# Seeding an accumulation bank from ScalarE in a Strassen-style up projection (one Trainium2 core)

## The chip, the core and the metric

The kernel runs on one core of a Trainium2 chip. The core has a matrix engine (TensorE, PE in the rows, with its weight loads as PEld), a vector engine (VectorE, DVE), an activation engine (ScalarE, ACT), GpSimd (POOL), and SyncE (SP), which here only starts transfers. Each engine runs its own instructions in order and waits for the others by semaphores. Matrix products land in PSUM, which holds eight banks of 128 x 512 fp32; everything else lives in SBUF or in HBM. The metric is the device time of one execution in microseconds (us).

## The reference

Three parts run one after the other on 3072 tokens of width 512: a retention layer, and two feed-forward networks of inner width 2048.

```python
for t in range(S):
    state = gamma * state + k_t v_t^T
    y[:, :, t] = scale * q_t state
x = y as (3072, 512)
h = x @ w_in;   g = h / (1 + exp(-1.702 * h));   x = g @ w_out       # moe, l = 0
h = x @ w_in2;  g = max(h, 0) ** 2;              out = g @ w_out2    # moe2, l = 1
```

All matrices are fp32. The kernel keeps that precision by splitting each operand into a high and a low part (fp32r) and taking three products: low weight by high x, high weight by high x, high weight by low x.

## The kernel before

**Stages.** The retention comes first. Then two blocks of 512 tokens go through the first network in the plain way. The other tokens go in *blocks* (l, n) of 1024 tokens (l is the network): (0,1), whose up projection is still plain, then (0,2), (1,0), (1,1), (1,2). Each block has an up stage and a down stage. The four blocks after (0,1) run their up stage in `up2`; all five run their down stage in `down2`.

**Seven products.** Both stages use a Strassen-Winograd scheme: a 2 x 2 block product is made of seven products instead of eight, from sums of quarters of the weights and of x. In `up2` the outer loop is over rounds p = 0 to 7 (NQ = 8), one for each strip of 128 inner columns, and one call past the end (p = 8) that finishes round 7. A product is six matmuls of 128 x 128 by 128 x 512. The quarters of the result, named 11, 12, 21 and 22, are SBUF tiles `g[q, p // 2]`, reached by `gt(q, p)`.

**The order in a round.** Product 1 goes into bank X, which ScalarE copies to quarter 11 (L882, through the helper at L864). Then products 4 and 3 of the round before finish quarters 21 and 12 (L887, L896); in round 0 there is no round before, and this part is skipped. Product 2 opens bank Y (L904, L905). VectorE adds Y to quarter 11 (L906, through the helper at L869). Product 6 accumulates onto X, copied to quarter 12 (L909); product 5 opens bank Z; product 7 accumulates onto X again, copied to quarter 22 (L913), to which Z is added (L914). The eight bank numbers stand in a deque: `bank` takes one from its left, and a free one goes back on its right.

**The activation.** `add` queues gelu, or relu and square, in `late`; the next `copy` on ScalarE runs what is queued, right behind itself. In blocks (1,1) and (1,2) VectorE does relu squared itself (L876). Quarter 21 is finished by product 4 alone and gets its activation straight from the bank (L890, L892, L893).

**What else is in the queues.** `background` (L903, L916) issues pieces of a weight maker: while (0,2) and (1,0) run, it makes the weight sums of the second network out of raw weights, with ScalarE scalings and casts (L129, L130, L383), VectorE sums, and GpSimd transfers to HBM (L346). `prepare` (L946, L947) splits operands of the down stage; it is called in rounds 6 and 7. SP fetches the weights of every product from HBM into eight slots (L761), each refilled when its product is through. `loads` (L1059) brings the next block's x from HBM at the start of a down stage. The order on every engine is the order of the program (`manual_schedule`).

Of the kernel before, what the change touches and what calls it, by code (L numbers as in the profile page):

```python
# [15 lines left out]
ACTF = mybir.ActivationFunctionType  # L16
# [44 lines left out]
def tile_retention_then_two_ffns(  # L61
# [10 lines left out]
    nc = tc.nc  # L72
# [336 lines left out]
    def background(us):  # L409

        credit[0] += us
        while acts:
            acts.popleft()()
        while credit[0] > 0:
            c = next(maker, None)
            if c is None:
                credit[0] = min(credit[0], 3.0)
                return
            credit[0] -= c
# [21 lines left out]
    with tc.manual_schedule():  # L441
# [310 lines left out]
        def fetch():  # L752
            while queue and len(fetched) < SLOTS:
                l, n, m, i, p = key = queue[0]
                if turn[0] % SLOTS >= len(wr_p):
                    return
                assert key[:1] + key[2:3] + key[4:] in made
                queue.popleft()
                t = wr_p[turn[0] % SLOTS].tile([P, 2, 256], F32R, tag="w", name="r{}_{}_{}_{}_{}".format(*key))
                turn[0] += 1  # L760
                nc.sync.dma_start(out=t.bitcast(F32), in_=kw[l][m][p][PRODUCT[i][0]])  # L761
                fetched[key] = t
# [21 lines left out]
        banks = deque(range(8))  # L784
# [48 lines left out]
        def thirds(m):  # L833

            t = g[12, m]
            v.tensor_tensor(out=t, in0=g[22, m], in1=t, op=ALU.subtract)

        def bank(name):
            k = banks.popleft()
            return ps_p[0].tile([P, TB], F32, tag=f"b{k}", name=name), k  # L840

        def matmul(a, w, b, start, stop):
            nc.tensor.matmul(a, w, b, start=start, stop=stop, skip_group_check=True)  # L843

        def up2(l, n, first):

            xb, yb, zb = {}, {}, {}
            late = deque()

            def product(i, p, a, start):  # L850
                s, b = PRODUCT[i]
                w = fetched.pop((l, n, 0, i, p)).rearrange("p k (h c) -> p k h c", h=2)
                for k in range(2):
                    hi, lo = w[:, k, 0], w[:, k, 1]
                    matmul(a, lo, xh[b][:, k], start and k == 0, False)
                    matmul(a, hi, xh[b][:, k], False, False)
                    matmul(a, hi, xl[b][:, k], False, k == 1)
                fetch()

            def gt(q, p):  # L860
                return g[q, p // 2][:, p % 2]

            def copy(t, a):
                nc.scalar.copy(out=t, in_=a)  # L864
                while late:
                    late.popleft()()

            def add(t, a):
                v.tensor_tensor(out=t, in0=a, in1=t, op=ALU.add)  # L869
                if l == 0:  # L870
                    late.append(lambda: nc.scalar.activation(out=t, in_=t, func=ACTF.Gelu_apprx_sigmoid))
                elif n == 0:
                    late.append(lambda: nc.scalar.activation(out=t, in_=t, func=ACTF.Relu))
                    late.append(lambda: nc.scalar.activation(out=t, in_=t, func=ACTF.Square))
                else:
                    v.scalar_tensor_tensor(out=t, in0=t, scalar=0.0, in1=t, op0=ALU.max, op1=ALU.mult)  # L876

            for p in range(NQ + 1):
                if p < NQ:
                    xb[p] = bank(f"X{l}_{n}_{p}")  # L880
                    product(1, p, xb[p][0], True)
                    copy(gt(11, p), xb[p][0])  # L882
                else:
                    next(first)
                if p > 0:
                    a, k = xb.pop(p - 1)
                    product(4, p - 1, a, False)  # L887
                    t = gt(21, p - 1)
                    if l == 0:
                        nc.scalar.activation(out=t, in_=a, func=ACTF.Gelu_apprx_sigmoid)  # L890
                    else:
                        nc.scalar.activation(out=t, in_=a, func=ACTF.Relu)  # L892
                        nc.scalar.activation(out=t, in_=t, func=ACTF.Square)  # L893
                    banks.append(k)
                    a, k = zb.pop(p - 1)
                    product(3, p - 1, a, False)  # L896
                    add(gt(12, p - 1), a)
                    banks.append(k)
                    if p == NQ - 1:
                        prepare(l, n)  # L900
                if p < NQ:
                    if (l, n) != blocks[-1] and p < NQ - 1:
                        background(BGUP[l])  # L903
                    yb = bank(f"Y{l}_{n}_{p}")  # L904
                    product(2, p, yb[0], True)  # L905
                    add(gt(11, p), yb[0])  # L906
                    banks.append(yb[1])
                    product(6, p, xb[p][0], False)
                    copy(gt(12, p), xb[p][0])  # L909
                    zb[p] = bank(f"Z{l}_{n}_{p}")  # L910
                    product(5, p, zb[p][0], True)
                    product(7, p, xb[p][0], False)
                    copy(gt(22, p), xb[p][0])  # L913
                    add(gt(22, p), zb[p][0])  # L914
                    if (l, n) != blocks[-1] and p < NQ - 1:
                        background(BGUP[l])  # L916
                if p == NQ:
                    while late:
                        late.popleft()()
                if p > 1 and p % 2 == 0:  # L920
                    thirds(p // 2 - 1)
                if p == NQ - 2:
                    prepare(l, n)
# [6 lines left out]
        def prepare(l, n):  # L930

            if not todo:
                return
            i, m = todo.popleft()
            k = places[0]
            places[0] += 1
            hi, lo = (
                pool.tile([P, 2, TB], F32R, tag=tag, name=f"gx{l}_{n}_{i}_{m}_{e}")
                for e, (pool, tag) in enumerate(
                    ((wa_p, "w0"),) * 2 if k < 3 else  # L940
                    ((wa_p, "w0"), (wb_p, "w0")) if k % 3 == 2 else ((hl_p, "hl"),) * 2
                )
            )

            src = g[{1: 11, 2: 21, 6: 11, 5: 11, 7: 12, 4: 21, 3: 22}[i], m]
            nc.scalar.copy(out=hi, in_=src)  # L946
            v.tensor_tensor(out=lo, in0=src, in1=hi, op=ALU.subtract)  # L947
            ready.append((i, m, hi, lo))
# [96 lines left out]
        for k, (l, n) in enumerate(blocks):  # L1045
            todo.extend((i, m) for i in ORDER for m in range(NQ // 2))
            gen = [iter(())]

            xt = []

            def loads(u):

                if k + 1 == len(blocks):
                    return
                t, i = divmod(u, 2)
                b, j = blocks[k + 1]
                if i == 0:
                    xt.append(block_tiles(f"xb{b}_{j}_{t}"))
                nc.gpsimd.dma_start(out=xt[t][i], in_=(xkept, ykept)[b][2 * j + t][:, 2 * i:2 * i + 2])  # L1059
                if u == 3:  # L1060
                    gen[0] = x_operands(*xt)

            rest = down2(l, n, loads, lambda: next(gen[0], None))
            if (l, n) == plain:
                up_plain()
            else:
                up2(l, n, rest)
            for _ in rest:
                pass
            for _ in gen[0]:  # L1070
                pass
            if (l, n) == (1, 0):
                assert next(maker, 0) == 0 and not acts
# [83 lines left out]
```

## Time and profile before

| | us |
|---|---|
| three runs of the kernel before | 1041.03, 1043.52, 1044.09 |
| their median | 1043.52 |
| the profiled execution | 1041.52 |
| its span, first to last instruction | 1039.8 |
| TensorE busy | 1028.8 (99%) |
| VectorE busy | 762.5 (73%) |
| ScalarE busy | 559.1 (54%) |
| HBM traffic | 263 GB/s over the span |

Matmuls overlap one another: one starts every 0.227 us and its row lasts 0.39 us, so TensorE's busy time counts rows that run together and is no measure of its peak. What holds TensorE up is better read from its waits. The other engines' busy times are averages over stages that differ; a stage's own share is read from windows of the timeline.

### The profile page before, as it was taken

The numbers are of one execution on the slowest core, as the hardware profiler recorded it, in microseconds if no ns is written. First come the engines' busy times: TensorE is split into PE (matmuls) and PEld (weight loads), VectorE is DVE, ScalarE is ACT, GpSimd is POOL, SyncE is SP. The second block draws the span as 40 slices with busy tenths as digits, with TensorE's granted clock in tenths as the row PEclk, the third lists the DMA queues.
The fourth block names the chain that finished last, engine by engine and source line by source line (L and its number), as shares of the span: only waits on it lengthen the run. The fifth ranks groups of instructions, "written<-read, shape, count | busy, mean of one in ns | idle before, by whom it ended". The sixth has DMA issues, their size and how long they took to land.

```text
span 1039.8 us, 15581 instructions
## 1 busy us (share of the span) xinstructions
PE 1028.8 (99%) x5602; PEld 849.1 (82%) x5602; DVE 762.5 (73%) x1059; ACT 559.1 (54%) x906; POOL 119.7 (12%) x183
## 2 busy tenths in 40 slices
PE   9999999999999999999999999999999999999998
PEld 6888888888888888888788888788888888888886
DVE  5798998798898888567787566887445986355953
ACT  4677775344766365556455688464233464234442
POOL 3121210111333000112000111000100001000000
PEclk9999999999999999999999999999999999999999
DMA  9995898865898867999867898767866667776664
GB/s 348 404 404 174 270 313 298 308 229 223 268 349 286 312 208 227 329 338 351 276 213 229 309 369 299 272 210 236 296 193 194 203 204 229 219 194 193 207 198 162
DMA packets 114637, 274.04 MB, mean 264 GB/s; under 512 B 12160, under 2 KB 12288, under 8 KB 114304
## 3 DMA queue, kind: packets, MB, share of 16 engines
q1 hardware_dynamic: 87008, 171.32, 50.0%
q0 software_dynamic: 26976, 100.67, 27.6%
q8 instruction: 45, 0.74, 0.3%
q10 hardware_dynamic: 576, 1.05, 0.3%
q14 instruction: 32, 0.26, 0.1%
HBM read 199.59 MB, written 73.40 MB: 263 GB/s over the span
## 4 chain that ended last, share of the span: by engine, by line
PE 82%; DMA 2%; DVE 0%; issue 0%
PE D L843 36%; PE X L843 16%; PE Z L843 8%; PE Y L843 4%; PE h L797 3%; PE h L795 3%; PE h L796 3%; DMA r<-kw 2%; PE y L676 2%; PE y L674 2%; PE y L675 2%; PE h L643 2%; PE h L645 1%; PE h L644 1%; DVE o L981 0%
## 5 line engine op out<-in xcount | busy, mean ns | idle before, releaser
L843 PE MATMUL D<-gx,r 128*128 128x512 f32 x1680 | 383.7, 390 | 2.9 <-DMA r<-kw 2.9
L843 PEld LDWEIGHTS D<-gx,r 128*128 128x128 f32 x1680 | 314.7, 188 | 70.8 <-DMA r<-kw 4.6
L947 DVE TENSOR_TENSOR gx<-g,gx 128x1024 fp32r<-128x1024 f32 x140 | 170.6, 1221 | 49.8 <-ACT gx L946 49.2
L946 ACT CAST gx<-g 128x1024 fp32r<-128x1024 f32 x140 | 145.1, 1050 | 110.2 <-PE D L843 97.4
L843 PE MATMUL X<-xh,r 128*128 128x512 f32 x512 | 157.7, 389 | 0.0
L864 ACT COPY g<-X 128x512 f32<-128x512 f32 x96 | 56.3, 586 | 154.6 <-PE X L843 154.4
L869 DVE TENSOR_TENSOR g<-Z,g 128x512 f32<-128x512 f32 x64 | 44.2, 691 | 123.0 <-ACT g L864 93.6
L843 PEld LDWEIGHTS X<-xh,r 128*128 128x128 f32 x512 | 96.0, 188 | 20.1 <-ACT g L864 0.2
L843 PE MATMUL X<-xl,r 128*128 128x512 f32 x256 | 99.6, 389 | 0.0
L843 PE MATMUL Z<-xh,r 128*128 128x512 f32 x256 | 78.8, 389 | 0.0
L843 PEld LDWEIGHTS Z<-xh,r 128*128 128x128 f32 x256 | 48.0, 188 | 10.0
L843 PEld LDWEIGHTS X<-xl,r 128*128 128x128 f32 x256 | 48.1, 188 | 10.0
L643 PE MATMUL h<-hl,w 128*128 128x512 f32 x128 | 50.2, 392 | 0.4 <-DVE w L167 0.4
L644 PE MATMUL h<-hl,w 128*128 128x512 f32 x128 | 49.9, 390 | 0.0
L645 PE MATMUL h<-hl,w 128*128 128x512 f32 x128 | 49.8, 389 | 0.0
L676 PE MATMUL y<-gl,w 128*128 128x512 f32 x128 | 49.8, 389 | 0.0
L674 PE MATMUL y<-gh,w 128*128 128x512 f32 x128 | 49.8, 389 | 0.0
L675 PE MATMUL y<-gh,w 128*128 128x512 f32 x128 | 49.8, 389 | 0.0
L795 PE MATMUL h<-hl,w 128*128 128x512 f32 x128 | 49.8, 389 | 0.0
L796 PE MATMUL h<-hl,w 128*128 128x512 f32 x128 | 49.8, 389 | 0.0
L797 PE MATMUL h<-hl,w 128*128 128x512 f32 x128 | 49.8, 389 | 0.0
L843 PE MATMUL Z<-xl,r 128*128 128x512 f32 x128 | 49.8, 389 | 0.0
(107 smaller groups left out, 1604.5 us busy)
## 6 DMA issues: line engine op xcount, KB each, us to landing
r<-kw SPq DMA_DIRECT2D x504, 256.0 KB, 3.0
kw<-wq POOLq DMA_DIRECT2D x32, 896.0 KB, 6.5
unit<-qkv SPq DMA_DIRECT2D x48, 512.0 KB, 9.0
raw<-w POOLq DMA_DIRECT2D x32, 512.0 KB, 6.3
kw<-wh POOLq DMA_DIRECT2D x16, 1024.0 KB, 4.7
kw<-w SPq DMA_DIRECT2D x16, 512.0 KB, 5.0
raw<-win POOLq DMA_DIRECT2D x16, 512.0 KB, 6.5
raw<-wout POOLq DMA_DIRECT2D x16, 512.0 KB, 7.2
```

Source lines behind the costliest of these rows:

```text
L643: nc.tensor.matmul(hp, lo[:, k], xh, start=(k == 0), stop=False)
L644: nc.tensor.matmul(hp, hi[:, k], xh, start=False, stop=False)
L645: nc.tensor.matmul(hp, hi[:, k], xl, start=False, stop=(k == KD - 1))
L674: nc.tensor.matmul(a, lo[:, e], gh, start=s0, stop=False)
L675: nc.tensor.matmul(a, hi[:, e], gh, start=False, stop=False)
L676: nc.tensor.matmul(a, hi[:, e], gl, start=False, stop=s1)
L795: nc.tensor.matmul(hp, lo[:, k], xh, start=(k == 0), stop=False)
L796: nc.tensor.matmul(hp, hi[:, k], xh, start=False, stop=False)
L797: nc.tensor.matmul(hp, hi[:, k], xl, start=False, stop=(k == KD - 1))
L843: nc.tensor.matmul(a, w, b, start=start, stop=stop, skip_group_check=True)
L946: nc.scalar.copy(out=hi, in_=src)
L947: v.tensor_tensor(out=lo, in0=src, in1=hi, op=ALU.subtract)
```

## The change

Product 1 goes into X as before, but ScalarE copies it into the bank of product 2, Y, which is now taken ahead of the copy. Product 2 no longer opens that bank: its first matmul accumulates onto what ScalarE wrote. ScalarE then reads the finished sum from Y and writes quarter 11 through gelu, or through relu and a square in place; VectorE's addition, its relu squared in blocks (1,1) and (1,2), and the queued activation of quarter 11 go.

```diff
                 if p < NQ:
                     xb[p] = bank(f"X{l}_{n}_{p}")
                     product(1, p, xb[p][0], True)
-                    copy(gt(11, p), xb[p][0])
+                    yb[p] = bank(f"Y{l}_{n}_{p}")
+                    copy(yb[p][0], xb[p][0])
                 else:
                     next(first)
@@
                 if p < NQ:
                     if (l, n) != blocks[-1] and p < NQ - 1:
                         background(BGUP[l])
-                    yb = bank(f"Y{l}_{n}_{p}")
-                    product(2, p, yb[0], True)
-                    add(gt(11, p), yb[0])
-                    banks.append(yb[1])
+                    a, k = yb.pop(p)
+                    product(2, p, a, False)
+                    t = gt(11, p)
+                    if l == 0:
+                        nc.scalar.activation(out=t, in_=a, func=ACTF.Gelu_apprx_sigmoid)
+                    else:
+                        nc.scalar.activation(out=t, in_=a, func=ACTF.Relu)
+                        nc.scalar.activation(out=t, in_=t, func=ACTF.Square)
+                    banks.append(k)
                     product(6, p, xb[p][0], False)
```

## Rows read from the trace of the kernel before

**Rows 1.** The page: span, then busy us, share of it, instructions.
```profile
span 1039.8 us, 15581 instructions
...
PE 1028.8 (99%) x5602; PEld 849.1 (82%) x5602; DVE 762.5 (73%) x1059; ACT 559.1 (54%) x906; POOL 119.7 (12%) x183
```

**Rows 2.** Waits of PE and, in 576:640, PEld: waiter, released by: us, times, longest.
```profile
PE D L843 <- DMA r<-kw: 2.9, 4, 1.0
...
PEld X L843 <- ACT g L864: 0.2, 1, 0.2
```

**Rows 3.** Chain that ended last, in order: start us, us, what.
```profile
422.82 1.36 PE Y L843 x6
...
432.34 1.36 PE Y L843 x6
...
492.21 10.23 DMA r<-kw
```

**Rows 4.** Groups by line and form: count, busy us, mean ns, idle before.
```profile
L864 ACT COPY g<-X 128x512 f32<-128x512 f32 x96 | 56.3, 586 | 154.6 <-PE X L843 154.4
...
L869 DVE TENSOR_TENSOR g<-Y,g 128x512 f32<-128x512 f32 x32 | 22.0, 687 | 4.4 <-PE Y L843 4.2
...
L437 ACT CAST hl<-x 128x512 fp32r<-128x512 f32 x12 | 6.5, 617 | 0.0
```

**Rows 5.** Timeline, round 0 of (0,2): start us, us, what, [idle before <-releaser].
```profile
422.43 0.39 PE L843 MATMUL X<-xl,r 128*128 128x512 f32 x1
...
422.65 0.62 PE L843 MATMUL Y<-xh,r 128*128 128x512 f32 x2
...
422.85 0.59 ACT L864 COPY g<-X 128x512 f32<-128x512 f32 x1 [8.69 <-PE X L843]
```

**Rows 6.** Timeline, ScalarE, round 0 of blocks (1,0) and (1,2).
```profile
577.10 0.59 ACT L864 COPY g<-X 128x512 f32<-128x512 f32 x1 [8.69 <-PE X L843]
...
884.40 0.59 ACT L864 COPY g<-X 128x512 f32<-128x512 f32 x1 [8.69 <-PE X L843]
```

**Rows 7.** Timeline, (1,0): ScalarE's copy, the weight load and matmul behind it.
```profile
630.60 0.57 ACT L864 COPY g<-X 128x512 f32<-128x512 f32 x1
...
631.22 0.30 PEld L843 LDWEIGHTS X<-xh,r 128*128 128x128 f32 x2 [0.18 <-ACT g L864]
...
631.30 0.65 PE L843 MATMUL X<-xh,r 128*128 128x512 f32 x2
```

**Rows 8.** Timeline: round 7 of (0,2), and a copy in (1,0).
```profile
488.82 0.58 ACT L864 COPY g<-X 128x512 f32<-128x512 f32 x1
...
489.29 0.62 PE L843 MATMUL Y<-xh,r 128*128 128x512 f32 x2
...
594.66 0.56 ACT L864 COPY g<-X 128x512 f32<-128x512 f32 x1
```

**Rows 9.** Timeline, (1,0): round 3's scaling and product 7; round 4's pair.
```profile
607.56 0.68 ACT L130 ACTIVATE raw<-raw 128x512 uint32<-128x512 uint32 x1
...
609.54 0.62 PE L843 MATMUL X<-xh,r 128*128 128x512 f32 x2
...
614.15 0.58 ACT L892 ACTIVATE g<-X 128x512 f32<-128x512 f32 x1
...
615.30 0.93 ACT L383 CAST wq<-w 128x896 fp32r<-128x896 f32 x1
```

**Rows 10.** Windows of the up stages of (1,0), (1,1): us, busy us, PEclk, DMA.
```profile
575.60:646.50 70.90, 70.90 (x314) 58.61 (x313) 47.08 (x88) 58.25 (x98) 13.33 (x19) 1.00 0.95 333
730.40:806.60 76.20, 76.20 (x338) 63.10 (x337) 38.59 (x53) 25.48 (x41) 2.98 (x6) 1.00 0.75 228
```

**Rows 11.** DMA issues in 480:490 and 490:494 (us to landing); timeline of GpSimd.
```profile
r<-kw SPq DMA_DIRECT2D x8, 256.0 KB, 5.8
...
r<-kw SPq DMA_DIRECT2D x3, 256.0 KB, 10.2
...
488.78 0.94 POOL L346 DMA_DIRECT2D kw<-wq  x1 [7.27 <-DVE wq L345]
489.72 2.18 POOL L1059 DMA_DIRECT2D xb<-ykept  x4
```

## The prediction

> **What bounds the kernel now.** I read the page's first part, then the table of who waited for whom, filtered to TensorE, then the chain of waits in order of time, and last the timeline around one up stage. The page [rows 1] shows TensorE busy for 99% of the span and ScalarE for 54%. Busy TensorE rows overlap, so that 99% proves little by itself. The waits do: the matmuls wait 2.9 us in total, always for a weight fetch, four times [rows 2], and in the up stages one weight load waits once, 0.2 us, for ScalarE. The chain [rows 3] shows the rest: product after product without a gap, 1.36 us each (six matmuls), and one round of seven products every 9.52 us (from the Y product of round 0 at 422.82 to that of round 1 at 432.34). So TensorE's stream sets the end. VectorE and ScalarE work beside it; taking work off VectorE gains nothing unless TensorE waited for it, and any wait put into the stream is added to the span in full.
>
> **Part by part.**
>
> *VectorE's additions of product 2.* 32 go, 22.0 us of VectorE [rows 4]; in blocks (1,1) and (1,2) the 16 in-place relu squared behind them go too. No wait of TensorE in [rows 2] names them: worth nothing on the path. The cover is TensorE's own stream.
>
> *The copy, now from bank to bank.* 32 copies stay on ScalarE and only their target moves. A copy out of PSUM takes 586 ns on average, a cast of the same size that reads SBUF 617 [rows 4]. No row writes PSUM from ScalarE. I bound it by 0.53 us (0.59 less twice the 31 ns that the memory read makes) and 0.69 us (VectorE's slowest operation on this size in [rows 4], rounded), and take 0.59, the row with the same source.
> The Trainium skill, "ScalarE: Activation LUTs", section "Step-by-step: what each stage is for", says that ScalarE writes PSUM faster than SBUF. "Perfetto Trace Analysis", section "Optimizing Scalar/DVE Operations", puts ScalarE's access overhead at 93 ns on SBUF and 51 on PSUM, with the profiled latency about twice that. By these, as an estimate, the copy would take some 0.5 us and the whole sum would be about 0.3 us smaller; only the read side of it is visible in this trace.
>
> *The new wait.* This is the part that costs. Before, product 2 opened its own bank and needed nothing from ScalarE. Now its first matmul must wait until the copy has landed. Queued behind that matmul is the whole of TensorE's stream, and everyone else waits for that.
> In rounds 1 to 7 products 4 and 3 of the round before lie between product 1 and product 2: 2.72 us of cover for a copy of 0.59. In round 0 there is no round before: product 2 follows product 1 directly, and there are four such rounds, one for each up stage in this form. The timeline of the first [rows 5]: the last matmul of product 1 starts at 422.43 and ends at 422.82, product 2 starts at 422.65, and ScalarE, idle for 8.69 us, starts the copy at 422.85, so it lands at 423.44. The same 8.69 us of idleness stands ahead of the copy in the other three ([rows 6] has two of them): no backlog makes it later. The restart is read from the one place where TensorE waits for a ScalarE copy today [rows 7]: the copy ends at 631.17, the weight load starts at 631.22 and the matmul at 631.30, 0.13 us after the copy. So product 2 would start at 423.44 + 0.13 = 423.57, in place of 422.65: **0.92 us in each of four places, 3.7 us**. Bounds: with a copy of 0.53, 0.86 each (3.4); with a copy of 0.69 and a whole weight load of 0.19 plus 0.05 ahead of the matmul, 1.13 each (4.5).
>
> *Rounds 1 to 7: is the copy ever late?* ScalarE also has the weight maker's work and the casts for the down stage ahead of it. I went through the 28 rounds. Only one ends after product 2 starts: round 7 of block (0,2), where maker work and a down cast stand ahead and the copy runs from 488.82 to 489.40, while product 2 starts at 489.29 [rows 8]. With the restart, 489.53: **0.24 us**. The next tightest copy, round 2 of (1,0), ends at 595.22 [rows 8], 0.72 us ahead of its product 2 (which starts three products and a round before the product 7 at 609.54 in [rows 9]: 609.54 - 4.08 - 9.52 = 595.94), and stays hidden.
>
> *Gelu or relu squared of quarter 11 moves ahead.* It ran on ScalarE behind the copy of quarter 12; now it stands ahead of that copy, and product 7 may overwrite its bank only when that copy is through. In l = 0 it is one operation and ScalarE waits for TensorE before nearly every copy: free. In blocks (1,1) and (1,2) it is 1.25 us of new ScalarE work a round, on an engine busy for 25.5 of 76.2 us [rows 10]: free. In block (1,0) ScalarE is busy for 58.25 of 70.90 us [rows 10], and there it is tight. Round 3 [rows 9]: the last scaling starts at 607.56 and gives way about 0.57 later, 608.13; the pair occupies 1.15 us (614.15 to 615.30, the same pair elsewhere); the copy then runs from 609.28 to 609.87, and product 7, which starts at 609.54 today, starts at 610.00: 0.46 us. By the same steps rounds 2, 4, 5 and 7 give 0.16, 0.08, 0.07 and about 0.1: 0.87 in all. Against that, the pair no longer makes the copy of quarter 22 late at the end of rounds 1 and 2, which gives back about 0.15 us in rounds 2 and 3: **0.6 us**, between 0.3 and 0.9.
>
> *Banks and queues.* Y's bank is taken three products earlier, but the banks come round in the same order and nothing in [rows 2] waits for a bank; SP's weight fetches and GpSimd's transfers keep their order: nothing.
>
> *Sum.* 3.7 + 0.24 + 0.6 = **4.5 us** on the profiled execution's 1041.52 us (span 1039.8 and 1.7 around it) gives 1046.0. That execution lies 2.0 below the median of the three runs; the middle of all four times shown is 1042.5. I put the sum on that: **1047.0 us**.
>
> **The rivals.**
>
> *The fetch waits swallow the stalls.* TensorE waits 2.9 us for weights at the start of the down stages behind (0,2) and (1,0) [rows 2]. If a stall ahead of them lets the fetches catch up, the time is given back: at most 2.9 us, so 1042.5 + 4.5 - 2.9 = 1044.1, not slower as far as can be measured. The mechanism is the transfers' backlog, and it decides from the point at which the late fetches land about 1 us sooner after their issue than the 10.2 us of [rows 3]. Against it: the fetches take 5.8 us in the middle of the stage and 10.2 only behind 490 [rows 11], when four loads of the next block's x have gone out at 489.72. The backlog is a burst, and the burst and the fetches both move along with TensorE's stream. A stall in round 0 cannot thin it. For it: the burst is issued before round 7's new 0.24 us stall ends, so that one may well be absorbed. Chance 0.2.
>
> *ScalarE becomes the bound in block (1,0).* If moving the pair ahead cost 0.46 us, as in round 3, in each of rounds 1 to 6 and a similar delay reached the copies for products 2, I would add 2 x 6 x 0.46 - 0.6 = 4.9: 1051.9. Against it: ScalarE is still idle for 12.65 us of that stage [rows 10], 1.3 us or more a round, so a backlog drains within about a round. Chance 0.07.
>
> *The unloaded VectorE gains time.* If the last weights made in a stage left for memory sooner, by a 0.69 us addition less, they would be clear of the burst, and both fetch waits would go without the stalls being absorbed: the same 2.9 us, and with the copy at its lower bound 1042.5 + 4.2 - 2.9 = 1043.8. Against it: the burst leaves GpSimd's queue right behind the last weights, 0.94 us after their issue at 488.78 [rows 11], so it would leave sooner with them. Chance 0.05.
>
> **How the numbers follow.** Forecast 0.68, the rivals 0.2, 0.07 and 0.05. About 0.3%, 3.1 us, is what a measurement of this kernel can tell from no change. The forecast's own span of 3.4 + 0 + 0.3 to 4.5 + 0.24 + 0.9 is 3.7 to 5.6, all beyond it, but the runs themselves scatter by 1.5 us, so I count a sixth of it as within. With nearly all of the second rival, slower gets 0.57 + 0.07 and a little of the first, 0.66; within 0.3% gets 0.31; faster 0.03. Range: down to 1043.5, where the first and third rivals lie, up to 1050.0, which is the upper bound 5.6 on the highest run shown.
>
> **What would show it.** In the trace after: a gap of about 0.9 us ahead of the first Y matmul in each up stage, four times, with the waits of TensorE naming ScalarE's copy, some 3.7 us; one gap of 0.2 us in round 7 of (0,2); small ones ahead of product 7 in (1,0); fetch waits still near 2.9 us; ScalarE's copy into Y between 0.53 and 0.69 us. The prediction is wrong if the round-0 gap is under 0.7 us, if waits for ScalarE come in the later rounds of every block, or if the fetch waits shrink by as much as the gaps add.

## The result, and the profile after

The changed kernel takes 1047.32 us (median of 5 runs, 1046.31 to 1050.63) against 1043.43 for the kernel before (5 runs, 1040.31 to 1044.09). The ratio is 1.0053 with a 95% interval of 1.0037 to 1.007: slower by 3.9 to 7.3 us. The forecast was 1047.0 and slower. The profiled execution took 1046.31 us, 4.8 over that of before.

The page, to set beside [rows 1] (span; busy us, share, instructions):

```profile
span 1044.5 us, 15555 instructions
...
PE 1030.2 (99%) x5602; PEld 848.1 (81%) x5602; DVE 731.3 (70%) x1011; ACT 579.4 (55%) x938; POOL 120.1 (11%) x183
```

TensorE executes the same 5602 matmuls. VectorE has lost 31.2 us of work and ScalarE gained 20.3; the span has grown by 4.7. The totals alone would let one expect the opposite, for the engine that lost work was the busier of the two. What counts is who is waited for. The waits of TensorE's matmuls and of its weight loads, to set beside [rows 2] (waiter, released by: us, times, longest):

```profile
PE Y L843 <- ACT Y L864: 2.6, 4, 0.7
PE D L843 <- DMA r<-kw: 2.6, 4, 1.2
...
PEld Y L843 <- ACT Y L864: 4.7, 5, 1.1
...
PEld X L843 <- ACT g L864: 1.4, 5, 0.5
```

The first row is new: four waits of almost 0.7 us for the copy into Y. The weight loads wait there too (third row), and a fifth time in round 7 of (0,2). The waits for weight fetches are what they were, 2.6 in place of 2.9. The last row, one wait of 0.2 before, is now five with 1.4 us: product 7 in block (1,0).

Round 0 of (0,2) in the timeline, to set beside [rows 5] (start us, us, what, [idle before <-releaser]):

```profile
422.63 0.39 PE L843 MATMUL X<-xl,r 128*128 128x512 f32 x1
423.06 0.57 ACT L864 COPY Y<-X 128x512 f32<-128x512 f32 x1 [8.69 <-PE X L843]
...
423.68 0.73 PE L843 MATMUL Y<-xh,r 128*128 128x512 f32 x2 [0.66 <-ACT Y L864]
...
424.25 0.39 PE L843 MATMUL Y<-xl,r 128*128 128x512 f32 x1
```

Product 1 ends at 423.02, the copy starts at once and lands at 423.63, and the matmul starts 0.05 us later. Before, the first Y matmul started 0.22 us after the last X matmul; now it is 1.05. There is a second, smaller loss: the first pair of matmuls takes 0.73 us instead of 0.62, because its weight loads have no earlier matmul to run beside: before they start at 422.43, with the last matmul of product 1, and now at 423.68, with the pair itself. The chain of waits has both (start us, us, what):

```profile
421.66 1.37 PE X L843 x6
423.06 0.58 ACT Y L864
423.68 1.66 PE Y L843 x6
425.34 1.36 PE X L843 x6
```

From the start of product 1 to the end of product 2 it is 425.34 - 421.66 = 3.68 us, against two products of 1.36 in [rows 3]: 0.96 us. The other three up stages have the same rows. Round 7 of (0,2) shows the short form, the copy landing at 490.56 where product 2 would have started at 490.47:

```profile
489.99 0.57 ACT L864 COPY Y<-X 128x512 f32<-128x512 f32 x1
...
490.62 0.73 PE L843 MATMUL Y<-xh,r 128*128 128x512 f32 x2
```

It costs 0.30 us (1.66 for the product in place of 1.36). Then block (1,0), round 3, to set beside [rows 9]:

```profile
610.27 0.67 ACT L130 ACTIVATE raw<-raw 128x512 uint32<-128x512 uint32 x1
610.83 0.57 ACT L911 ACTIVATE g<-Y 128x512 f32<-128x512 f32 x1
611.44 0.63 ACT L912 ACTIVATE g<-g 128x512 f32<-128x512 f32 x1
611.98 0.57 ACT L864 COPY g<-X 128x512 f32<-128x512 f32 x1
...
612.60 0.73 PE L843 MATMUL X<-xh,r 128*128 128x512 f32 x2
```

Scaling, pair (relu and square), copy, product 7, each starting where the one ahead gives way: the order that the prediction worked out. The matmul ahead of product 7 started at 612.10. One starts every 0.227 us, so product 7 would have started at 612.33 instead of 612.60.

By blocks, from one first X matmul to the next: (0,2) 155.77 us against 154.25, (1,0) 155.90 against 154.81, (1,1) 153.41 against 152.49, and (1,2) with the tail 157.92 against 156.96. These are 1.52, 1.09, 0.92 and 0.96, in all 4.5, and 0.2 lies ahead of the first. The up stages alone, from product 1 of round 0 to product 4 of round 7, are longer by 1.25, 1.65, 0.96 and 0.96, in all 4.8; behind them the waits for weight fetches are 0.3 shorter.

### The profile page after: what moved, and what is told of

Same layout as the page of the kernel before. It is cut to its first block, busy times and chain, and to the rows that moved or that the text cites. A ratio compares the mean times of both kernels' runs of the same rounds, so it can differ in the third digit from the quotient of the medians.

```text
span 1044.5 us, 15555 instructions
## 1 busy us (share of the span) xinstructions
PE 1030.2 (99%) x5602; PEld 848.1 (81%) x5602; DVE 731.3 (70%) x1011; ACT 579.4 (55%) x938; POOL 120.1 (11%) x183
## 3 DMA queue, kind: packets, MB, share of 16 engines
q10 hardware_dynamic: 576, 1.05, 0.3%
## 4 chain that ended last, share of the span: by engine, by line
PE 81%; DMA 2%; ACT 1%; DVE 0%; issue 0%
PE D L843 36%; PE X L843 16%; PE Z L843 8%; PE Y L843 4%; PE h L796 3%; PE h L795 3%; PE h L797 3%; DMA r<-kw 2%; PE y L675 2%; PE y L674 2%; PE y L676 2%; PE h L643 2%; PE h L644 1%; PE h L645 1%; ACT Y L864 0%; DVE g L836 0%
## 5 line engine op out<-in xcount | busy, mean ns | idle before, releaser
L843 PE MATMUL D<-gx,r 128*128 128x512 f32 x1680 | 383.7, 390 | 2.6 <-DMA r<-kw 2.6
L843 PEld LDWEIGHTS D<-gx,r 128*128 128x128 f32 x1680 | 314.7, 188 | 70.4 <-DMA r<-kw 4.3
L843 PE MATMUL X<-xh,r 128*128 128x512 f32 x512 | 158.1, 390 | 0.1
L843 PEld LDWEIGHTS X<-xh,r 128*128 128x128 f32 x512 | 95.7, 188 | 21.1 <-ACT g L864 1.4
L843 PE MATMUL X<-xl,r 128*128 128x512 f32 x256 | 99.6, 389 | 0.0
L843 PE MATMUL Z<-xh,r 128*128 128x512 f32 x256 | 78.8, 389 | 0.0
L864 ACT COPY g<-X 128x512 f32<-128x512 f32 x64 | 37.6, 587 | 61.9 <-PE X L843 60.0
L843 PEld LDWEIGHTS Z<-xh,r 128*128 128x128 f32 x256 | 48.0, 188 | 10.0
L843 PEld LDWEIGHTS X<-xl,r 128*128 128x128 f32 x256 | 48.0, 188 | 10.0
L843 PE MATMUL Z<-xl,r 128*128 128x512 f32 x128 | 49.8, 389 | 0.0
```

## The experiments

The theory: TensorE's stream now waits for a ScalarE copy that nothing covers in round 0 (0.96 us, four times), and for ScalarE's queue at five tight places. The rivals: that seeding a bank costs something in every round; that the gap is a fixed restart cost; and that stalls and fetch waits stand in for each other. In what follows "over" is always over the kernel before as run beside it.

**Round 0 as before.** Round 0 takes the old path, rounds 1 to 7 the new one.

```diff
-                    yb[p] = bank(f"Y{l}_{n}_{p}")
-                    copy(yb[p][0], xb[p][0])
+                    if p > 0:
+                        yb[p] = bank(f"Y{l}_{n}_{p}")
+                        copy(yb[p][0], xb[p][0])
+                    else:
+                        copy(gt(11, p), xb[p][0])
...
```

The part left out (`...`) lets product 2 of round 0 open its bank again, with VectorE's addition behind it.

> Rounds 1 to 7 of all four up stages as in the changed kernel, round 0 as before (quarter 11 copied to SBUF, product 2 opens its bank, VectorE adds). Theory: the uncovered copy in round 0 costs 0.96 us four times and the rest about 1.0 us (0.30 in round 7 of (0,2), 0.65 ahead of product 7 in (1,0)), so this kernel lies about 1 us over the kernel before (ratio 1.001), and the trace has no wait of TensorE for ScalarE in round 0. Rival, that the seeded bank makes every product 2 dearer: 28 of 32 rounds keep it, so some 4 us over the kernel before.

Measured: 1045.07 us (8 runs) against 1042.16, ratio 1.0029 (1.0015 to 1.0042). Its weight loads' waits (waiter, released by: us, times, longest):

```profile
PEld X L843 <- ACT g L864: 1.4, 5, 0.5
...
PEld Y L843 <- ACT Y L864: 0.4, 1, 0.4
```

No matmul waits for ScalarE any more, and the weight loads' waits that are left are those of round 7 and of product 7. The trace says what the theory says of round 0; its span is 1041.6, 1.8 over that of before. The time, 1.6 to 4.4 us over, lies above the 1 us that the theory expected and does not by itself exclude the rival's 4; what speaks against the rival is that the waits are gone. I come back to this under the control.

**Round 0 alone.** The same edit with `p == 0` in place of `p > 0`.

> Only round 0 of the four up stages as in the changed kernel, rounds 1 to 7 as before. Theory: four gaps of 0.96 us, 3.8 us over the kernel before (ratio 1.0037), with waits of TensorE for ScalarE's copy in the same four places and no others. Rival, a cost in every round: about an eighth of the change's, 0.6 us.

Measured: 1045.99 us against 1042.16, ratio 1.0052 (1.0033 to 1.0071).

```profile
PE Y L843 <- ACT Y L864: 2.6, 4, 0.7
```

The same row as in the changed kernel. Four seeded rounds of 32 cost about what all 32 cost: the rival that spreads the cost over the rounds expected 0.6 us, and falls.

**The copy made twice.**

```diff
                     yb[p] = bank(f"Y{l}_{n}_{p}")
+                    if p == 0:
+                        nc.scalar.copy(out=yb[p][0], in_=xb[p][0])
                     copy(yb[p][0], xb[p][0])
```

> The changed kernel with the copy into the bank of product 2 made twice in round 0. Theory: the gap holds the whole copy, so each of the four grows by one copy's pace, 0.48 to 0.57 us: 1.9 to 2.3 us over the changed kernel, 6.6 to 7.0 over the kernel before (ratio 1.0064 to 1.0067). Rival, that the gap is a fixed cost of TensorE's restart and of the hand-over: no growth, 4.7 over the kernel before.

Measured: 1051.34 us, ratio 1.0091 (1.0074 to 1.0109), above the ratio that was expected. The row of waits, and round 0 of (0,2) in the timeline:

```profile
PE Y L843 <- ACT Y L864: 5.0, 4, 1.3
```

```profile
426.04 0.57 ACT L884 COPY Y<-X 128x512 f32<-128x512 f32 x1 [8.69 <-PE X L843]
426.64 0.57 ACT L864 COPY Y<-X 128x512 f32<-128x512 f32 x1
...
427.26 0.73 PE L843 MATMUL Y<-xh,r 128*128 128x512 f32 x2 [1.26 <-ACT Y L864]
```

The four waits grow by 2.4 us, 0.60 each. The second copy starts 0.60 after the first, when that one has ended, and not the 0.48 at which the queue otherwise goes on. So the copy's length is in the gap, and the rival of a fixed cost falls. The rest of the excess in the traced execution is not the copy's: block (0,2) starts at 424.48 there and at 421.50 in the changed kernel, 3.0 us later, behind a retention that no edit touched (the last section shows what happened in it).

**The copy covered.** Product 1 of round 0 and its copy are issued ahead of the last step of the down stage before; all 32 rounds still seed. `start`, whose text is left out here, makes product 1 and the copy.

```diff
...
+            for _ in range(27 if (l, n) == plain else 26):
+                next(rest)
+            if k + 1 < len(blocks):
+                start(*blocks[k + 1])
             for _ in rest:
                 pass
```

> The changed kernel with product 1 of round 0 and its copy issued ahead of the last step of the down stage before (12 matmuls, 2.72 us of cover), its weights fetched two places earlier. Theory: the copy of 0.57 us is covered, the four gaps go and about 1 us stays over the kernel before (0.30 and 0.65): ratio 1.001. Rival, that the seeding costs by itself: all 32 rounds still seed, so the 4.7 us stay (1.0045).

The timeline around the first such copy, TensorE's rows and then ScalarE's:

```profile
419.35 0.39 PE L848 MATMUL X<-xl,r 128*128 128x512 f32 x1
419.58 2.88 PE L848 MATMUL D<-gx,r 128*128 128x512 f32 x12
...
422.30 0.62 PE L848 MATMUL Y<-xh,r 128*128 128x512 f32 x2
...
419.78 0.57 ACT L859 COPY Y<-X 128x512 f32<-128x512 f32 x1 [5.97 <-PE X L848]
```

The copy runs beside the 12 down matmuls and the Y matmuls follow in step, 0.62 for the pair. The gap is gone with the seeding in place. The span is 1041.1, 1.3 over that of before; the runs give 1045.60 us, ratio 1.0035 (1.0023 to 1.0047), which is 2 us more than that and again above the theory's 1 us.

**A control, and the change without waits.** Round 0 as before and the covered copy came out some 2 us higher than their traces. So the kernel before was run once more, beside itself, and with it a version in which every wait found so far is ordered away: round 0 as before, the activation back behind the copy of quarter 12, and the down cast of round 6 behind round 7's copy.

> The kernel before, unchanged, run as a candidate of its own. It measures what a comparison of a kernel with itself gives, since the two kernels that should lie 1 us over the kernel before came out 2.9 and 3.4 over it while their traces show 1.3 to 1.8. Theory (the comparison adds nothing): ratio 1.000, within 0.001. Rival (a kernel that runs as a candidate comes out some 1.5 to 2 us longer): ratio 1.0015 to 1.002.

> Seeding in rounds 1 to 7 only; round 0 as before; the activation of quarter 11 back behind the copy of quarter 12; the down cast of round 6 behind round 7's copy into Y. Theory: no wait of TensorE for ScalarE is left in the up stages but the 0.2 us weight load of before, so the time is that of the kernel before, ratio 1.000. Rival (seeding costs something that the waits don't show): 1 to 3 us over it, ratio 1.001 to 1.003, with the trace free of such waits.

The control gives 1043.52 against 1042.28 us, ratio 1.0012 (0.9998 to 1.0027). Its interval holds 1.000 as well as the rival's 1.0015 to 1.002. Its trace has a span of 1041.8, 2.0 over that of the first trace of the same kernel. So neither a comparison of times nor one of spans can tell 1 us from 0 or 2.

The version without waits gives 1042.67, ratio 0.9989 (0.9971 to 1.0008). Its matmuls never wait for ScalarE. The waits of its weight loads put one of 0.7 us to ScalarE, which the timeline and the chain of waits in block (1,1) don't bear out:

```profile
743.71 0.61 ACT L918 ACTIVATE g<-Y 128x512 f32<-128x512 f32 x1
...
744.77 0.30 PEld L843 LDWEIGHTS X<-xh,r 128*128 128x128 f32 x2 [0.65 <-ACT g L918]
```

```profile
735.06 9.61 DMA r<-kw
744.67 0.14 issue
744.81 4.33 PE X L843 x18
```

The operation named ends at 744.32; what landed last, at 744.67, is a weight fetch. So no wait for ScalarE is left in the up stages, and seeding has no cost of its own in sight: of the 4.7 us nothing measurable is left when the waits are gone. Taking 28 additions off VectorE is worth nothing either.

**The activation behind the copy again.** The changed kernel, with quarter 11's activation queued in `late` (`finish_11` holds the lines taken out).

```diff
-                    if l == 0:
-                        nc.scalar.activation(out=t, in_=a, func=ACTF.Gelu_apprx_sigmoid)
-                    else:
...
+                    late.append(finish_11)
                     banks.append(k)
```

> The changed kernel with the activation of quarter 11 put back behind the copy of quarter 12, where it ran before. Theory: the waits ahead of product 7 in (1,0), 0.65 us in all, go; the four gaps of 0.96 us and the 0.30 us in round 7 of (0,2) stay, so 4.1 us over the kernel before (ratio 1.004). Rival, that ScalarE's backlog in (1,0) comes from the maker and not from the order: the waits ahead of product 7 stay, 4.7 us.

The chain of waits of block (1,0), first of the changed kernel, then of this one, from product 7 of rounds 3, 4 and 5 on (start us, us, what: three products of X, 4.08 us where nothing waits):

```profile
612.60 4.37 PE X L843 x18
...
622.41 4.18 PE X L843 x18
...
632.03 4.19 PE X L843 x18
```

```profile
616.55 4.08 PE X L843 x18
...
626.07 4.08 PE X L843 x18
...
635.59 4.08 PE X L843 x18
```

All waits ahead of product 7 are gone; from the start of product 1 of round 0 to that of product 6 of round 7 it is 70.32 us, against 71.03 in the changed kernel. The order was the cause, not the maker's load by itself. The time is 1048.39 us, ratio 1.0058 (1.0039 to 1.0077); it tells nothing on 0.65 us.

**VectorE makes the copy.** Round 0's copy is `v.tensor_copy` in place of ScalarE's.

> The changed kernel with round 0's copy into the bank made by VectorE. Theory: the gap holds the copy's own length, and VectorE is idle there; a copy of 0.69 us (its operations of this size that read PSUM) in place of 0.57 makes each of the four gaps 0.12 us longer, 0.5 us in all. Rival, that VectorE's way into PSUM is the quicker one: the gaps shrink.

The copies into Y by line (min, median and max ns, first and last start), and the row of waits:

```profile
L884 DVE COPY Y<-X x4: 698/698/700, 422.7 to 889.4; 128x512 f32<-128x512 f32 x4
...
L864 ACT COPY Y<-X x28: 570/570/610, 430.6 to 954.5; 128x512 f32<-128x512 f32 x28
```

```profile
PE Y L843 <- DVE Y L884: 3.2, 4, 0.8
```

Each wait grows by 0.13 to 0.15 us, as 698 ns against 570 makes it. The time of the one run is 1047.70 us.

**The other wait, with and without the change.** The next block's x loads go from GpSimd's queue to SyncE's, between the weight fetches and two steps apart: first in the kernel before, then in the changed kernel and in the version without waits.

```diff
-                nc.gpsimd.dma_start(out=xt[t][i], ...)
+                nc.sync.dma_start(out=xt[t][i], ...)
@@
-                    if u < 4:
-                        loads(u)
+                    if u in (2, 4, 6, 8):
+                        loads(u // 2 - 1)
```

> The kernel before with the next block's four x loads moved from GpSimd's queue to SyncE's, one every second step of the down stage, between the weight fetches. It tests what the fetch waits at the start of the down stages come from. Theory: the burst of x loads makes them, so the 2.9 us of waits on weight fetches shrink below 1 us and the span by some 2 us (ratio 0.998). Rival: the maker's last weights alone fill the transfers, the waits stay (1.000), or the x loads now delay the fetches behind them in the same queue (over 1.000).

> The changed kernel with the x loads on SyncE's queue as in the run before. Theory: the two effects are independent; the fetch waits of 2.6 us go, the waits for ScalarE (4 x 0.96, 0.30, 0.65) stay, so it lies some 4.8 us over the kernel before with the same x loads, or 1.5 us over the kernel before (ratio 1.0015). Rival (the first rival of the prediction: stalls and fetch waits partly stand in for each other): with the fetch waits gone the stalls cost more than before, ratio 1.003 or more.

> Seeding in rounds 1 to 7 with the waits for ScalarE ordered away, and the x loads on SyncE's queue. Theory: TensorE's stream has no wait left in the up stages in either form, so seeding buys nothing and the time is that of the kernel before with the x loads moved, ratio 0.997 to the kernel before. Rival (taking 27 us off VectorE shortens something): below 0.996.

The kernel before with this edit takes 1038.83 us, ratio 0.9968 (0.9952 to 0.9983); it beats both kernels. Its waits hold no weight fetch at all, and the three fetches behind 490 take half the 10.2 us of [rows 11]:

```profile
PE sc L487 <- DMA unit<-qkv: 3.9, 3, 2.1
PE warm L466 <- DVE warm_sb L455: 1.2, 1, 1.2
PE sc L487 <- DVE hl L526: 0.6, 2, 0.3
```

```profile
r<-kw SPq DMA_DIRECT2D x3, 256.0 KB, 5.1
```

The changed kernel with it takes 1043.33, ratio 1.0008 (0.9996 to 1.002; nine executions, 1043.01 to 1043.78), and the version without waits 1038.20, ratio 0.9963 (0.9949 to 0.9977), the last two beside the same runs. A tenth execution of the changed kernel with this edit, the one that was traced, took 3396.11 us: its matmuls of 128 x 512 lasted about 1 us in place of 0.39. Why is not known, and it is left out. That the fetch waits are gone from the other nine is taken over from the traces of the two other kernels, which have none. Then the waits for ScalarE cost 1043.33 - 1038.20 = 5.1 us, near the 4.8 that the trace's terms make: the two kinds of wait add up, as far as the runs can tell. And the version without waits is as fast as the kernel before with the same edit: the lighter VectorE buys nothing. The edit moves the loads to another queue and also spaces them; which of the two removes the waits was not separated.

**The up stages by themselves.** The traces tell more than the times, for most of the scatter lies outside the up stages. From product 1 of round 0 to product 4 of round 7, the four stages add up to 304.7 us in the kernel before. The table has what each trace lies over that, beside what the theory's terms (0.96 four times, 0.30, 0.65) make for it.

| trace | over, us | by the terms |
|---|---|---|
| the kernel before again; the kernel before with the x loads moved | 0.0; 0.0 | 0; 0 |
| round 0 as before | 1.65 | 0.95 |
| round 0 alone | 3.8 | 3.8 |
| the copy made twice | 7.3 | 4.8 + 1.9 to 2.3 |
| the copy covered, less the 12 down matmuls now inside each stage (2.72) | 1.05 | 0.95 |
| the activation behind the copy | 4.1 | 4.1 |
| VectorE makes the copy | 5.4 | 4.8 + 0.5 |
| without waits; the same with the x loads moved | 0.45; -0.05 | 0; 0 |

The two that stand out, 1.65 and 0.45, each have a late weight fetch in block (1,1), worth 0.65 and 0.5 us there; that of the version without waits is shown above.

## Why the prediction was right, step by step

*What bounds the kernel.* Right. The difference of the two traces lies in gaps of TensorE's stream, and 31 us less work on VectorE show nowhere, least of all in the version that seeds without waits. One reading was too wide: the matmuls' 2.9 us of waits, "always for a weight fetch", are those of L843. In the retention they wait as well, among others for its loads:

```profile
PE sc L487 <- DMA unit<-qkv: 1.4, 4, 0.5
```

These waits differ from execution to execution (below).

*The copy in round 0.* Forecast 0.92 us, measured 0.96, four times; with round 0 as before the matmuls' waits go, with the copy doubled they grow by a copy. That the two figures are so close is partly luck, for two parts of the term were off and nearly cancelled: the hand-over took 0.05 us and not 0.13, and the first pair of matmuls 0.11 longer. The row of [rows 7] has only 0.03 of that (0.65 in place of 0.62), for there the load waited 0.18 us and earlier matmuls were still under way.
The copy's length, taken as 0.59 us between 0.53 and 0.69, is 0.57. ScalarE's other copies from X in the same trace write SBUF (min, median and max ns, first and last start):

```profile
L864 ACT COPY g<-X x64: 567/589/589, 426.7 to 961.2; 128x512 f32<-128x512 f32 x64
L864 ACT COPY Y<-X x32: 570/570/595, 423.1 to 953.1; 128x512 f32<-128x512 f32 x32
```

So the rule in the Trainium skill, "ScalarE: Activation LUTs", section "Step-by-step: what each stage is for", that ScalarE writes PSUM faster than SBUF, holds in direction, by 19 ns of the medians. The estimate of 0.5 us from the figures in the Trainium skill, "Perfetto Trace Analysis", section "Optimizing Scalar/DVE Operations", was too short; the row decides.

*Rounds 1 to 7.* One late copy was named, round 7 of (0,2), with 0.24 us; it is the fifth wait in the rows, with 0.30.

*Product 7 in (1,0).* Forecast 0.6 us in rounds 2, 3, 4, 5 and 7, measured 0.65 for the stage: in the chain about 0.11, 0.39, 0.10 and 0.11 in rounds 2 to 5, less some 0.05 that the kernel before had. In round 7 the weight load waits too, the fifth in the row, but the chain has no more than 0.02 there. The experiment with the order put back takes all of them away.

*The sum.* 4.5 us against 4.7 in the span, 4.8 in the up stages, and 1047.0 against 1047.32. That the time agrees to 0.3 us is luck: the prediction started from 1042.5, 0.9 below the median of the five runs of the kernel before, and the changed kernel's own runs spread over 4.3 us.

*The rivals.* The fetch waits did not swallow the stalls: 2.6 us in place of 2.9, and without them the stalls cost the same. The prediction named the cause, the burst of x loads, and the waits go when the loads are spaced out in another queue. ScalarE did not become the bound in (1,0). The third rival, that VectorE's gain would free the fetches, did not come about.

*What stays open.* Round 0 as before and the covered copy should lie 1 us over the kernel before; the runs put them 1.6 to 4.4 and 2.4 to 4.9 us over. Their up stages are as the theory has them, but for the late fetch (table above), and in the covered copy's trace the waits for fetches in the down stages are 3.6 us in place of 2.9.

The rest goes with TensorE's granted clock, which is on record as a mean for each execution. Where it is 0.998 or less the execution is longer, in the kernel before too: of its 27 runs beside the control, eight are such, 1045.2 us on average, and the other 19 take 1041.7. Four of the eight runs of round 0 as before and six of the ten of the covered copy are such, against 2 of the 20 beside them; the others lie 1.8 and 2.2 us over the others of before (1043.7 and 1044.1 against 1041.9). In the two traces at 0.998 the clock fell in the retention, which no edit touched: the first matmul behind it starts 3.3 and 3.8 us later than in the trace of before, wait and clock together. Where it fell in the untraced executions is not on record. Nor is it known why such executions came so often there, though the control, with no edit, has four in ten. The retention's waits for its loads also vary from trace to trace: 2.2 us in the changed kernel, 1.1 in the version without waits and 4.0 with the activation put back. Why the weight fetch in (1,1) came late in two of the traces is open.

## What to carry to other kernels

On an engine that streams without gaps, moving work off a second engine is worth nothing, and a new dependency is worth what its cover lacks: look for the round in which the products that cover it don't exist, usually the first of a loop. Work that is moved ahead in an in-order queue delays what stood there; find the reader of that, and its slack. The waits that the stream already has are the better target: here the gaps behind a burst of loads were worth 3 us, by moving the loads into the queue that paces the stream and spacing them between its fetches. And when a term is smaller than the scatter of the times, compare the lengths of the edited stages in the traces.

## What the runs showed of the hardware

TensorE's granted clock fell in the retention in two of the traces, those of the copy made twice (shown) and of the activation behind the copy. The matmuls had waited about 2 us for a load, and then the lower of the clock's two levels, 1.2 GHz, was granted for 3.4 us; in the windows the columns are us, busy us of PE, PEld, DVE, ACT and POOL, granted clock, DMA share, GB/s, and the wait follows from the timeline:

```profile
70.00:72.00 2.00, 1.31 (x38) 1.00 (x33) 2.00 (x4) 2.00 (x8) 0.00 (x0) 1.00 1.01 401
72.00:74.00 2.00, 0.81 (x8) 0.84 (x9) 0.53 (x1) 0.83 (x4) 0.00 (x0) 0.80 1.02 408
74.00:78.00 4.00, 4.00 (x62) 3.54 (x60) 2.57 (x3) 0.47 (x2) 2.11 (x3) 0.67 0.96 373
```

```profile
73.19 1.22 PE L487 MATMUL sc<-unit 64*128 64x128 f32 x8 [1.88 <-DMA unit<-qkv]
```

The kernel before with the x loads moved had a wait of 2.1 us there and no fall in the clock, so a wait of this length is no sure sign. The gaps of 0.7 us in the up stages were not followed by one: the clock is 1.00 throughout them.

Two ScalarE copies from one bank into another, one right behind the other, start 0.60 us apart, against 0.46 to 0.52 for such a copy and the next operation on another target. Whether it is the common target or the common source that holds the second back was not tested.
